# A gated mix of feature-map linear attention and a spatial gating unit: PE transposes for the first rows, v scaled in place of the key features, one PSUM pool, and a written TensorE order

## The chip, the cores and the metric

The kernel runs on one core of one Trainium2 chip. The metric is the time of one execution on the device in microseconds (us). PE is the engine of the matmuls, DVE, ACT and POOL are the vector, scalar and GpSimd engines, SP issues most of the transfers. Each engine runs its own instructions in order and waits for the others on semaphores.

## What is computed

x is 2048 x 512. Branch A is linear attention with 32 heads of 16 columns: softmax features of q and k (of +k w_phi and of -k w_phi), a sum of features times v over all rows, and a quotient. Branch B is a gated unit with 688 columns a half, whose second half is normalized and mixed over the rows. A gate per row mixes both.

```python
# A
phi_k = concat([softmax(pk), softmax(-pk)])      # pk = k @ w_phi, per head
kv = einsum('bhsf,bhsd->bhfd', phi_k, v); z = einsum('bhsf->bhf', phi_k)
o = einsum('bhqf,bhfd->bhqd', phi_q, kv) / (einsum('bhqf,bhf->bhq', phi_q, z) + 1e-6)
a = o @ wo
# B
z = gelu(x @ w_in); z1 = z[..., :688]; z2 = layernorm(z[..., 688:])
b = (z1 * (w_sp @ z2 + b_sp)) @ w_out
out = g * a + (1 - g) * b                        # g = sigmoid(sum(x * gate_w))
```

## The kernel before

Rows are worked on in 16 tiles of 128 (tt). The program has three stages. **z**: the x rows come transposed by DMA into xT (lines 92 to 106). In four chunks of four tiles, z2_tile multiplies the tile with the second half of w_in (and with gate_w as one more column, whose result DVE copies to glog), ACT takes the gelu, DVE the mean and variance; z1_tile does the first half; z2_norm normalizes the four tiles, with the power on POOL. zp, the PSUM result, has three buffers of two banks, and a buffer is free again when ACT's gelu and DVE's copy of the gate column have read it. DVE also casts bT (line 215), a bias that a DMA at the end of a long row of transposes on SP brings.

**Fold and kv**: w_phi is multiplied into wq and wk (lines 217 to 236), so that one product gives the exponents. For each tile kv_tile computes k and v, the exps of k and -k (ek), their sums a head (zk), the inverse (rk) and phik = ek rk; v is copied to vz with a column of ones behind it; kv_acc adds phik times vz into kvacc, which holds three banks through the stage. pq_tile does a fourth of the exps of q.

**Output**: gg_half multiplies the rows of w_sp with z2 in two halves of 344 columns (gp), and DVE forms ucat; attn_tile forms the quotient from eq and kvz (the masked kvacc); o and ucat are transposed by DMA (oT, uT); ba_tile adds both products (ba_ps), ACT scales and a DMA stores.

A scheduler of the framework sets the order of the instructions on every engine. PSUM has pools psA (z), psB (kv), psC (output) and psF throughout; psC begins where psB has ended.

## Time and profile before

| what | value |
|---|---|
| median of 3 runs | 237.82 us (237.62 to 238.41) |
| profiled execution | 236.93 us |
| its span, first to last instruction | 235.2 us |
| granted PE clock, mean | 0.993 |
| gp matmuls, 512 | 81.1 us busy, 313 ns each |
| z matmuls, 256 | 41.4 us busy, 324 ns each |
| wait of z for xT | 10.6 us of PE idle |

The span is what the trace covers; the rest of the execution's time lies around it. Busy times overlap on pipelined matmuls: a duration of 313 ns does not mean that one starts every 313 ns. What a matmul costs is read from the spacing of starts. In a row of the timeline the first number is the start and the second the duration in us; "x4" counts instructions merged into one row, and the bracket tells for how long the engine was idle ahead of it and what ended that. In rows of the groups the numbers are the total busy time, and the mean of one in ns.

### The profile page before, as it was taken

To read this page: it belongs to the slowest core of one execution; us is meant where nothing else is said; L and a number is where in the kernel's file an instruction comes from. 1 tells how busy PE (TensorE), PEld (TensorE's weight loads), DVE (VectorE), ACT (ScalarE), POOL (GpSimd) and SP (SyncE) were. 2 spreads that over 40 slices of the span, in tenths; PEclk is the share of its full clock that TensorE was granted. 3 is DMA by queue.
4 is the path that set the end of the run, shared out by engine and by line. 5 is a ranking of instruction groups with operands and counts; after the bars stand their busy time and mean duration, and the time that the engine had idled before them with its cause. 6 is when DMAs were issued, how large, how long until landed. Compare 5 with 4: busy or idle time off the path is not lost.

```text
span 235.2 us, 3568 instructions
## 1 busy us (share of the span) xinstructions
PE 212.9 (91%) x1412; PEld 127.9 (54%) x1412; DVE 149.0 (63%) x335; ACT 82.1 (35%) x133; POOL 9.9 (4%) x38
## 2 busy tenths in 40 slices
PE   0289999969999999995999999999999999999953
PEld 0046666645455555553675666666666566665611
DVE  0035747677999999997177745577455775556750
ACT  0126666694998888880001011110111101111011
POOL 7002021020000000000000000000000000000000
PEclk9999999999999999998899999999999999999999
DMA  7999999999900000000014234222333213322141
GB/s 139 203 220 256 253 189 283 241 200 267 261 3 0 0 3 0 0 0 3 1 34 84 52 78 81 56 52 51 78 78 59 55 47 79 81 57 54 48 100 45
DMA packets 72688, 22.29 MB, mean 95 GB/s; under 512 B 67888, under 2 KB 72672, under 8 KB 72672
## 3 DMA queue, kind: packets, MB, share of 16 engines
q1 hardware_dynamic: 71008, 20.64, 42.6%
q10 hardware_dynamic: 1632, 1.43, 3.2%
q8 instruction: 11, 0.18, 0.3%
q14 instruction: 5, 0.04, 0.1%
q0 software_dynamic: 32, 0.00, 0.0%
HBM read 3.18 MB, written 2.10 MB: 22 GB/s over the span
## 4 chain that ended last, share of the span: by engine, by line
PE 62%; DVE 28%; DMA 6%; issue 2%; ACT 1%; SPq 1%; POOLq 0%; DVEq 0%; POOL 0%; ACTq 0%
PE gp L371 32%; PE zp L172 14%; DVE phik L273 8%; PE ba_ps L391 8%; DVE zk L266 7%; PE ba_ps L389 5%; DMA xT<-in_A_x_dram 5%; DVE rk L271 4%; PE at L335 3%; DVE bn_83 L184 1%; DVE wk_p L236 1%; DVE wq_p L236 1%; DMA oT<-o 1%; DVE m L356 1%; DVE z2all L201 1%
## 5 line engine op out<-in xcount | busy, mean ns | idle before, releaser
L371 PE MATMUL gp<-z2all,wspT 128*128 128x344 bf16 x512 | 81.1, 313 | 0.8 <-DVE kvz L319 0.8
L371 PEld LDWEIGHTS <-wspT 128*128 128x128 bf16 x512 | 50.1, 99 | 26.8 <-issue 0.9
L393 ACT ACTIVATE ob<-ba_ps,g_inv 128x512 bf16<-128x512 f32 x16 | 11.0, 687 | 115.8 <-PE ba_ps L391 115.8
L172 PE MATMUL zp<-w_in,xT 128*128 128x344 bf16 (+1 forms) x256 | 41.4, 324 | 10.8 <-DMA xT<-in_A_x_dram 10.6
L172 PEld LDWEIGHTS <-xT 128*128 128x128 bf16 x256 | 25.6, 101 | 28.0 <-DMA xT<-in_A_x_dram 11.2
L391 PE MATMUL ba_ps<-w_out_t,uT 128*128 128x512 bf16 x96 | 23.3, 379 | 0.0
L273 DVE TENSOR_TENSOR phik<-ek,rk 128x1024 bf16<-128x1024 bf16 x16 | 19.6, 1223 | 1.3
L356 DVE TENSOR_TENSOR m<-at,r 128x1024 f32<-128x1024 f32 x16 | 19.6, 1224 | 0.5
L266 DVE TENSOR_REDUCE zk<-ek 128x64 f32<-128x1024 bf16 x16 | 19.3, 1209 | 0.0
L389 PE MATMUL ba_ps<-wo_t,oT 128*128 128x512 bf16 x64 | 16.6, 380 | 2.6 <-DMA oT<-o 2.6
L376 DVE SCALAR_TENSOR_TENSOR ucat_96<-gp,bT,z1all 128x344 bf16<-128x344 f32 x12 | 6.9, 571 | 18.8 <-PE gp L371 18.8
L181 ACT ACTIVATE z2all<-zp 128x688 bf16<-128x688 f32 x16 | 11.9, 744 | 15.2 <-PE zp L172 15.2
L253 PE MATMUL k_ps<-wk_p,xT 128*128 128x512 bf16 x64 | 16.9, 378 | 0.0
L256 PE MATMUL v_ps<-wv_sb,xT 128*128 128x512 bf16 x64 | 16.7, 379 | 0.0
L294 PE MATMUL pq<-xT,wq_p 128*128 128x512 bf16 x64 | 16.6, 379 | 0.0
L391 PEld LDWEIGHTS <-uT 128*128 128x128 bf16 x96 | 9.4, 98 | 11.2
L182 DVE COPY glog<-zp 128x1 f32<-128x1 f32 x16 | 2.5, 158 | 20.0 <-ACT z2all L181 19.8
L184 DVE BATCH_NORM_STATS2 bn_83<-z2all 128x6 f32<-128x344 bf16 x32 | 14.9, 501 | 0.0
L189 ACT ACTIVATE z1all<-zp 128x688 bf16<-128x688 f32 x16 | 11.7, 744 | 6.7 <-PE zp L172 6.7
L376 DVE SCALAR_TENSOR_TENSOR ucat_97<-gp,bT,z1all 128x344 bf16<-128x344 f32 x10 | 5.7, 570 | 13.0 <-PE gp L371 13.0
L376 DVE SCALAR_TENSOR_TENSOR ucat_98<-gp,bT,z1all 128x344 bf16<-128x344 f32 x10 | 5.7, 570 | 11.9 <-PE gp L371 11.9
L283 PEld LDWEIGHTS <-phik 128*128 128x128 bf16 x128 | 8.6, 98 | 6.1 <-DVE phik L273 2.8
(113 smaller groups left out, 197.4 us busy)
## 6 DMA issues: line engine op xcount, KB each, us to landing
out_dram<-ob SPq DMA_DIRECT2D x16, 128.0 KB, 1.9
w_in<-in_B_w_in_dram ACTq DMA_DIRECT2D x4, 172.0 KB, 4.3
w_in<-in_B_w_in_dram ACTq DMA_DIRECT2D x1, 688.0 KB, 10.2
w_out_t<-in_B_w_out_dram SPq DMA_DIRECT2D x1, 640.0 KB, 4.7
wv_sb<-in_A_wqkv_dram SPq DMA_DIRECT2D x1, 512.0 KB, 4.2
wo_t<-in_A_wo_dram SPq DMA_DIRECT2D x1, 512.0 KB, 5.2
oT<-o SPq DMA_TRANSPOSE x16, 2.5
uT<-ucat_96 SPq DMA_TRANSPOSE x6, 2.8
```

The source lines that it names most:

```text
L172: nc.tensor.matmul(zp[:, j, 0:n], lhsT=lhsT, rhs=w_in[:, dt, c0 + j * HF:c0 + j * HF + n], start=(dt == 0), stop=(dt == NDT - 1),)
L184: nc.vector.bn_stats(out=bn6[:, tt, j, :], in_=z2v[:, j, :])
L253: nc.tensor.matmul(k_ps[:, :], lhsT=xT[:, dt, t0:t0 + P], rhs=wk_p[:, dt, :], start=(dt == 0), stop=(dt == NDT - 1))
L256: nc.tensor.matmul(v_ps[:, :], lhsT=xT[:, dt, t0:t0 + P], rhs=wv_sb[:, dt, :], start=(dt == 0), stop=(dt == NDT - 1))
L266: nc.vector.tensor_reduce(out=zk[:, :], in_=ek[:].rearrange("p a (h e) -> p (a h) e", e=DH), axis=AX.X, op=ALU.add,)
L273: nc.vector.tensor_tensor(out=phik[:, :].rearrange("p (h e) -> p h e", e=DH), in0=ek[:].rearrange("p a (h e) -> p (a h) e", e=DH), in1=rk[ ...
L294: nc.tensor.matmul(pq[:, :], lhsT=wq_p[:, dt, g * P:(g + 1) * P], rhs=xT[:, dt, c0:c0 + CH], start=(dt == 0), stop=(dt == NDT - 1),)
L356: nc.vector.tensor_tensor(out=m[:].rearrange("p a (g h d) -> p (a g) h d", g=NG, d=DH), in0=at[:, :, :, 0:P].rearrange("p a g (h d) -> p ( ...
L371: nc.tensor.matmul(gp[:, :], lhsT=wspT[:, st, tt * P:(tt + 1) * P], rhs=z2all[:, st, j * HF:(j + 1) * HF], start=(st == 0), stop=(st == NT ...
L376: nc.vector.scalar_tensor_tensor(out=ucat[tt % NU][:, j * HF:(j + 1) * HF], in0=gp[:, :], scalar=bT[:, tt:tt + 1], in1=z1all[:, tt, j * HF ...
L389: nc.tensor.matmul(acc[:, :], lhsT=oT[:, g, :], rhs=wo_t[:, g, :], start=(g == 0), stop=False)
L391: nc.tensor.matmul(acc[:, :], lhsT=uT[:, ft, :], rhs=w_out_t[:, ft, :], start=False, stop=(ft == NFT - 1))
```

## The change

x rows 0 to 511 are loaded as they are (xs) and transposed on PE against an identity that DVE builds; gate_w is loaded as four rows and transposed on PE too. w_in becomes two tiles, loaded in pieces on SP and ACT. Eight matmuls on zeros stand first on PE. The folds stand between the z products of the last chunk, and every second result is copied by ACT. In the kv stage ek goes to kv_acc as it is; v is multiplied with rk once for each sign (vr, two DVE instructions from PSUM), and rk itself, copied by POOL, takes the place of the column of ones, so a kvacc block has 136 columns for 129. From kv to the end one pool psM serves all: four banks for k, v, pq, gp and the output products, four for kvacc and then at. The order on PE is the order of the code. The first gp half stands ahead of the last kv_acc; at of a tile follows its own gp halves, except for the last, where it stands between them. Stores go from ACT, and the last one is cut in two.

```diff
-    w_in = early.tile([P, NDT, F + 1], BF16, name="w_in")
+    w_z1 = early.tile([P, NDT, FH], BF16, name="w_z1")
+    w_z2 = early.tile([P, NDT, WP], BF16, name="w_z2")
...
-    NVZ = 4
-    vzs = [pers.tile([P, NG, P + 2], BF16, name=f"vz{i}") for i in range(NVZ)]
...
+    nc.vector.memset(warm[:], 0.0)
+    nc.vector.memset(ones32[:], 1.0)
...
+    for q in range(4):
+        qs = slice(32 * q, 32 * q + 32)
+        nc.vector.tensor_tensor(
+            out=ident[qs, qs], in0=ramp[qs, 0, :], in1=ramp[qs, 1, :], op=ALU.is_equal)
+    nc.gpsimd.dma_start(out=gaterow[:, :], in_=gate_w.rearrange("(dt p) -> dt p", p=P))
+    nc.sync.dma_start(out=xs[:, 0, :], in_=x2[0:P, :])
+    load_z2w(nc.scalar, 0)
+    load_z2w(nc.sync, 1)
+    load_z2w(nc.scalar, 2)
+    nc.sync.dma_start(out=xs[:, 1, :], in_=x2[P:2 * P, :])
+    load_z2w(nc.sync, 3)
+    nc.scalar.dma_start(
+        out=xs[:, 2:4, :], in_=x2[2 * P:4 * P, :].rearrange("(i p) d -> p i d", p=P))
+    for h in range(2):
+        nc.sync.dma_start(
+            out=w_z1[:, 2 * h:2 * h + 2, :], in_=w_in_v[:, 2 * h:2 * h + 2, 0:FH])
+    for i in range(4, 8):
+        nc.sync.dma_start_transpose(out=xT[:, :, i * P:(i + 1) * P], in_=x2[i * P:(i + 1) * P, :])
...
+    nc.scalar.dma_start(out=wphiE[:, :, :], in_=A_w_phi.rearrange("h e f -> e h f"))
...
-    def z_mm(tt, c0, w):
+    def z_mm(tt, wt, w, mid=None):
         zp = psA.tile([P, 2, CH], FP32, name="zp")
         for dt in range(NDT):
+            if dt == 2 and mid is not None:
+                mid()
...
+                    zp[:, j, 0:n], lhsT=lhsT, rhs=wt[:, dt, j * HF:j * HF + n],
...
-    def z2_tile(tt):
-        zp = z_mm(tt, FH, FH + 1)
+    def z2_tile(tt, mid=None):
+        zp = z_mm(tt, w_z2, FH + 1, mid)
...
-        zp = z_mm(tt, 0, FH)
+        zp = z_mm(tt, w_z1, FH)
...
-    for c in range(NCH):
-        ts = list(range(c * 4, c * 4 + 4))
-        for tt in ts:
-            z2_tile(tt)
-        for tt in ts:
-            z1_tile(tt)
-        z2_norm(ts)
-
-    nc.vector.tensor_copy(out=bT[:, :], in_=bT_bf[:, :])
...
+    def warm_up(n):
+        wp = psF.tile([P, CH], FP32, name="wp", tag="pq", bufs=2)
+        for _ in range(n):
+            nc.tensor.matmul(wp[:, :], lhsT=warm[:, 0:P], rhs=warm[:, :], start=True, stop=True)
+
+    def x_T(i):
+        tp = psF.tile([P, NDT, P], BF16, name="tp", tag="pq", bufs=2)
+        for dt in range(NDT):
+            nc.tensor.transpose(tp[:, dt, :], xs[:, i, dt * P:(dt + 1) * P], ident[:, :])
+        nc.vector.tensor_copy(out=xT[:, :, i * P:(i + 1) * P], in_=tp[:, :, :])
+
+    def gate_T():
+        gt = psF.tile([P, NDT], BF16, name="gt", tag="pq", bufs=2)
+        nc.tensor.transpose(gt[:, :], gaterow[:, :], ident[0:NDT, 0:NDT])
+        for dt in range(NDT):
+            nc.vector.tensor_copy(out=w_z2[:, dt, FH:FH + 1], in_=gt[:, dt:dt + 1])
+
+    def wphi_fold():
+        wps = psF.tile([P, NDT, P], FP32, name="wps", tag="pq", bufs=2)
+        for kc in range(NDT):
+            nc.tensor.matmul(
+                wps[:, kc, :], lhsT=eexp[:, :],
+                rhs=wphiE[:, kc * 8:(kc + 1) * 8, :].rearrange("e h f -> e (h f)"),
+                start=True, stop=True,
+            )
+        nc.vector.tensor_tensor(
+            out=wphi[:, :, :], in0=wps[:, :, :],
+            in1=mask_bd[:, None, :].to_broadcast([P, NDT, P]), op=ALU.mult,
+        )
+
...
+        if dt % 2 == 0:
+            nc.scalar.copy(out=dst[:, dt, :], in_=fps[:, :])
+        else:
             nc.vector.tensor_copy(out=dst[:, dt, :], in_=fps[:, :])
 
+    with tc.manual_schedule(engines={mybir.EngineType.PE}):
+        warm_up(8)
+        x_T(0)
+        gate_T()
+        for i in range(4):
+            z2_tile(i, (lambda k=i + 1: x_T(k)) if i < 3 else None)
+        for c in range(NCH):
+            ts = list(range(c * 4, c * 4 + 4))
+            last = c == NCH - 1
+            for tt in ts:
+                if c > 0:
+                    z2_tile(tt)
+                if last:
+                    fold(1, tt % 4)
+            for tt in ts:
+                z1_tile(tt)
+                if last:
+                    fold(0, tt % 4)
+            z2_norm(ts)
+            if c == NCH - 2:
+                wphi_fold()
...
+    psM = ctx.enter_context(
+        tc.tile_pool(name="psM", bufs=1, space=bass.MemoryType.PSUM, reuse_waits="tile"))
...
-    psB_cm = tc.tile_pool(name="psB", bufs=1, space=bass.MemoryType.PSUM, reuse_waits="tile")
-    psB = psB_cm.__enter__()
-    kvacc = [psB.tile([P, 3, P + 1], FP32, name=f"kvacc{i}") for i in range(3)]
-
-    def kv_tile(tt):
-        t0 = tt * P
-        k_ps = psB.tile([P, D], FP32, name="k_ps", bufs=2)
-        v_ps = psB.tile([P, D], FP32, name="v_ps", bufs=1)
+    kvacc = [psM.tile([P, NG, 256], FP32, name=f"kvacc{a}", tag="kvat", bufs=2) for a in range(2)]
...
+    def mm_tile():
+        return psM.tile([P, CH], FP32, name="mm", tag="mm", bufs=4)
+
+    def k_tile(tt):
+        k_ps = mm_tile()
...
-        vz = vzs[tt % NVZ]
-        nc.scalar.activation(
-            out=vz[:, :, 0:P], in_=v_ps[:, :].rearrange("p (g d) -> p g d", g=NG), func=AF.Copy,
-        )
+        ek = work.tile([P, 2, D], BF16, name="ek", bufs=4)
+        for a in range(2):
+            nc.scalar.activation(out=ek[:, a, :], in_=k_ps[:, :], func=AF.Exp, scale=1.0 - 2.0 * a)
...
-        phik = work.tile([P, 8 * P], BF16, name="phik", bufs=3)
...
+        return ek, rk
+
+    def v_tile(tt, rk):
+        v_ps = mm_tile()
+        for dt in range(NDT):
...
+        vr = work.tile([P, 2, NG, P + 8], BF16, name="vr", bufs=3)
+        nc.gpsimd.tensor_copy(
+            out=vr[:, :, :, P:P + 8], in_=rk[:].rearrange("p (a g h) -> p a g h", a=2, g=NG))
+        for a in range(2):
+            nc.vector.tensor_tensor(
+                out=vr[:, a, :, 0:P].rearrange("p g (h d) -> p g h d", d=DH),
+                in0=v_ps[:, :].rearrange("p (g h d) -> p g h d", g=NG, d=DH),
+                in1=rk[:, a * H:(a + 1) * H].rearrange("p (g h) -> p g h", g=NG)[:, :, :, None]
+                .to_broadcast([P, NG, 8, DH]),
+                op=ALU.mult,
+            )
+        return vr
+
+    def kv_acc(tt, ek, vr):
+        for a in range(2):
+            for g in range(NG):
+                nc.tensor.matmul(
+                    kvacc[a][:, g, 0:P + 8], lhsT=ek[:, a, g * P:(g + 1) * P], rhs=vr[:, a, g, :],
+                    start=(tt == 0 and g % 2 == 0), stop=(tt == NT - 1),
+                    skip_group_check=True,
+                )
...
-    pend = []
-    for tt in range(NT):
-        pend.append((tt,) + kv_tile(tt))
-        pq_tile(tt // 4, tt % 4)
-        if len(pend) > 2:
-            kv_acc(*pend.pop(0))
-    for p_ in pend:
-        kv_acc(*p_)
...
+    def kvz_evac():
+        for a in range(2):
+            nc.vector.tensor_tensor(
+                out=kvz[:, a * NG:(a + 1) * NG, 0:P], in0=kvacc[a][:, :, 0:P],
+                in1=mask_bd[:, None, :].to_broadcast([P, NG, P]), op=ALU.mult,
+            )
+            nc.vector.scalar_tensor_tensor(
+                out=kvz[:, a * NG:(a + 1) * NG, P:P + 8], in0=kvacc[a][:, :, P:P + 8],
+                scalar=0.5e-6, in1=mask8[:, None, :].to_broadcast([P, NG, 8]),
+                op0=ALU.add, op1=ALU.mult,
+            )
...
-        at = psC.tile([P, 2, NG, 256], FP32, name="at", bufs=1)
+        at = [psM.tile([P, NG, 256], FP32, name=f"at{a}", tag="kvat", bufs=2) for a in range(2)]
+        sd = work.tile([P, 2, NG, 16], FP32, name="sd")
...
-        sd = work.tile([P, 2, NG, 16], FP32, name="sd")
-        nc.vector.tensor_copy(out=sd[:], in_=at[:, :, :, P:P + 16])
+            nc.vector.tensor_copy(out=sd[:, a], in_=at[a][:, :, P:P + 16])
...
-        m = work.tile([P, 2, D], FP32, name="m", bufs=1)
-        nc.vector.tensor_tensor(
-            out=m[:].rearrange("p a (g h d) -> p (a g) h d", g=NG, d=DH),
-            in0=at[:, :, :, 0:P].rearrange("p a g (h d) -> p (a g) h d", d=DH),
-            in1=r[:].rearrange("p a g h -> p (a g) h")[:, :, :, None].to_broadcast([P, 8, 8, DH]),
-            op=ALU.mult,
-        )
+            nc.vector.tensor_tensor(
+                out=m[:, a].rearrange("p (g h d) -> p g h d", g=NG, d=DH),
+                in0=at[a][:, :, 0:P].rearrange("p g (h d) -> p g h d", d=DH),
+                in1=r[:, a][:, :, :, None].to_broadcast([P, NG, 8, DH]),
+                op=ALU.mult,
+            )
...
+        if tt < NT - 1:
+            nc.scalar.activation(out=ob[:, :], in_=acc[:, :], func=AF.Copy, scale=g_inv[:, tt:tt + 1])
+            nc.scalar.dma_start(out=out2[tt * P:(tt + 1) * P, :], in_=ob[:, :])
+        else:
+            hd = D // 2
+            nc.scalar.activation(out=ob[:, 0:hd], in_=acc[:, 0:hd], func=AF.Copy, scale=g_inv[:, tt:tt + 1])
+            nc.scalar.dma_start(out=out2[tt * P:(tt + 1) * P, 0:hd], in_=ob[:, 0:hd])
+            nc.vector.tensor_scalar(
+                out=ob[:, hd:D], in0=acc[:, hd:D], scalar1=g_inv[:, tt:tt + 1], scalar2=None, op0=ALU.mult)
+            nc.sync.dma_start(out=out2[tt * P:(tt + 1) * P, hd:D], in_=ob[:, hd:D])
+
+    nc.vector.tensor_copy(out=bT[:, :], in_=bT_bf[:, :])
...
-    for tt in range(NT):
-        gg_half(tt, 0)
-        if tt >= 1:
-            oTs[tt - 1] = attn_tile(tt - 1)
-        gg_half(tt, 1)
-        uTs[tt] = u_T(tt)
-        if tt == NT - 1:
-            oTs[tt] = attn_tile(tt)
-        if tt >= 2:
-            ba_tile(tt - 2, uTs.pop(tt - 2), oTs.pop(tt - 2))
-    for tt in (NT - 2, NT - 1):
-        ba_tile(tt, uTs.pop(tt), oTs.pop(tt))
-
-    psC_cm.__exit__(None, None, None)
+    with tc.manual_schedule(engines={mybir.EngineType.PE}):
+        ks = {0: k_tile(0)}
+        pend = []
+        for tt in range(NT):
+            if tt + 1 < NT:
+                ks[tt + 1] = k_tile(tt + 1)
+            ek, rk = ks.pop(tt)
+            pend.append((tt, ek, v_tile(tt, rk)))
+            pq_tile(tt // 4, tt % 4)
+            if len(pend) > 1:
+                kv_acc(*pend.pop(0))
+        nc.scalar.activation(out=g_el[:, :], in_=glog[:, :], func=AF.Exp)
+        nc.vector.tensor_scalar(out=g_1p[:, :], in0=g_el[:, :], scalar1=1.0, scalar2=None, op0=ALU.add)
+        nc.vector.reciprocal(out=g_inv[:, :], in_=g_1p[:, :])
+        gg_half(0, 0)
+        kv_acc(*pend.pop(0))
+        kvz_evac()
+        work_cm.__exit__(None, None, None)
+        work = ctx.enter_context(tc.tile_pool(name="workC", bufs=2, reuse_waits="tile"))
+        gg_half(0, 1)
+        uTs[0] = u_T(0)
+        oTs[0] = attn_tile(0)
+        for tt in range(1, NT):
+            gg_half(tt, 0)
+            if tt == NT - 1:
+                oTs[tt] = attn_tile(tt)
+            gg_half(tt, 1)
+            uTs[tt] = u_T(tt)
+            if tt < NT - 1:
+                oTs[tt] = attn_tile(tt)
+            if tt >= 2:
+                ba_tile(tt - 2, uTs.pop(tt - 2), oTs.pop(tt - 2))
+        for tt in (NT - 2, NT - 1):
+            ba_tile(tt, uTs.pop(tt), oTs.pop(tt))
 
```

Where the instructions stand now is shown at three places, first on DVE at the end of the first z chunk. Before (xT is written by DMA; z2all is the normalization of tiles 0 to 3, bT the cast, glog the gate copy of tile 4):

```order
L184 BN_STATS bn_83<-z2all 128x6
L185 BN_AGGR mv<-bn_83 128x2
L201 TENSOR_SCALAR z2all<-z2all,mv,rstd 128x688 x4
L215 CAST bT<-bT_bf 128x16
L182 COPY glog<-zp 128x1
L184 BN_STATS bn_83<-z2all 128x6 x2
```

After (the copy to xT empties the PE transpose of tile 3):

```order
L244 COPY xT<-tp 128x4x128
L213 BN_AGGR mv<-bn_84 128x2
L210 COPY glog<-zp 128x1
L212 BN_STATS bn_84<-z2all 128x6 x2
L229 TENSOR_SCALAR z2all<-z2all,mv,rstd 128x688 x4
L459 CAST bT<-bT_bf 128x16
```

The copies for xT came in ahead; the cast of bT stands where it stood, between the normalization and the gate copy of tile 4.

On ACT, the last z chunk. Before, the folds are not ACT's (g_el is the gate's exp, vz the copy of v):

```order
L312 ACT_TABLE_LOAD
L312 ACTIVATE g_el<-glog 128x16
L189 ACT_TABLE_LOAD
L189 ACTIVATE z1all<-zp 128x688 x4
L262 ACTIVATE vz_92<-v_ps 128x4x128
L259 ACT_TABLE_LOAD
L259 ACTIVATE ek<-k_ps 128x512
```

After:

```order
L276 CAST wk_p<-fps 128x512
L209 ACTIVATE z2all<-zp 128x688
L473 ACT_TABLE_LOAD
L473 ACTIVATE g_el<-glog 128x16
L217 ACT_TABLE_LOAD
L217 ACTIVATE z1all<-zp 128x688
L276 CAST wq_p<-fps 128x512
L217 ACTIVATE z1all<-zp 128x688 x2
L276 CAST wq_p<-fps 128x512
L217 ACTIVATE z1all<-zp 128x688
L323 ACT_TABLE_LOAD
L323 ACTIVATE ek<-mm 128x512 x4
```

Two fold copies came in between the gelus; the two loads around the gate's exp stayed; the exps of two k tiles follow at once.

On DVE, the start of the kv stage and its period. Before:

```order
L236 CAST wq_p<-fps 128x512 x4
L266 TENSOR_REDUCE zk<-ek 128x64
L271 RECIPROCAL rk<-zk 128x64
L273 TENSOR_TENSOR phik<-ek,rk 128x1024
L266 TENSOR_REDUCE zk<-ek 128x64
```

After:

```order
L325 TENSOR_REDUCE zk<-ek 128x64 x2
L330 RECIPROCAL rk<-zk 128x64 x2
L342 TENSOR_TENSOR vr<-mm,rk 128x4x128 x2
L325 TENSOR_REDUCE zk<-ek 128x64
L342 TENSOR_TENSOR vr<-mm,rk 128x4x128
L330 RECIPROCAL rk<-zk 128x64
L342 TENSOR_TENSOR vr<-mm,rk 128x4x128
```

Two tiles' zk and rk now precede the first vr, and later a vr of the tile before stands between zk and rk.

125 lines of the change are left out of this document (42 added, 83 removed).

## The prediction

> **What bounds the kernel now.** First the page's busy shares and slices, to see which engine is full in which stage.
>
> ```profile
> PE 212.9 (91%) x1412; PEld 127.9 (54%) x1412; DVE 149.0 (63%) x335; ACT 82.1 (35%) x133; POOL 9.9 (4%) x38
> PE   0289999969999999995999999999999999999953
> DVE  0035747677999999997177745577455775556750
> ```
>
> A slice is 5.88 us. PE is full except in the first three slices, near slice 9 (the fold), at slice 18 (the end of the kv stage) and in the last two. DVE is full beside PE in slices 9 to 17. So there is time to win only at the seams, and in the kv stage only if both engines get shorter. The timeline, engine by engine, gives the seams, each row as start, duration, instruction and the wait before it.
>
> ```profile
> 12.88 5.29 PE L172 MATMUL zp<-w_in,xT 128*128 128x344 bf16 x20 [5.28 <-DMA xT<-in_A_x_dram]
> 109.42 8.84 PE L371 MATMUL gp<-z2all,wspT 128*128 128x344 bf16 x48 [0.79 <-DVE kvz L319]
> 113.62 0.57 DVE L376 SCALAR_TENSOR_TENSOR ucat_96<-gp,bT,z1all 128x344 bf16<-128x344 f32 x1 [3.00 <-PE gp L371]
> 118.75 4.67 PE gp L371 x32
> 226.45 1.04 PE L389 MATMUL ba_ps<-wo_t,oT 128*128 128x512 bf16 x4 [2.08 <-DMA oT<-o]
> 229.28 1.04 PE L389 MATMUL ba_ps<-wo_t,oT 128*128 128x512 bf16 x4 [0.49 <-DMA oT<-o]
> ```
>
> PE starts z in earnest at 12.88. The first 16 gp matmuls run from 109.42 to about 113.55 (DVE takes their result at 113.62), 4.13 us, where the chain of waits has 32 in 4.67, so 2.33 for 16. At the end PE waits 2.08 and 0.49 for oT.
>
> **The start.** PE transposes replace the DMA transposes for rows 0 to 511, so z2 of tile 0 can begin as soon as plain loads land, far before 12.88. But all that is gained up to tile 7 hangs on one DVE row, and it did not move.
>
> ```profile
> 12.47 3.92 SPq L104 DMA_TRANSPOSE xT<-in_A_x_dram  x2
> 20.85 0.59 SPq L108 DMA_DIRECT2D wv_sb<-in_A_wqkv_dram  x1
> 21.49 1.13 SPq L112 DMA_TRANSPOSE bT_bf<-in_B_b_sp_dram  x1
> 25.49 0.17 DVE L215 CAST bT<-bT_bf 128x16 f32<-128x16 bf16 x1 [1.26 <-DMA bT_bf<-in_B_b_sp_dram]
> 25.75 0.16 DVE L182 COPY glog<-zp 128x1 f32<-128x1 f32 x1
> 28.50 0.74 ACT L181 ACTIVATE z2all<-zp 128x688 bf16<-128x688 f32 x1 [0.43 <-PE zp L172]
> 43.81 0.74 ACT L181 ACTIVATE z2all<-zp 128x688 bf16<-128x688 f32 x1 [0.44 <-PE zp L172]
> ```
>
> The cast of bT stands on DVE between the normalization of tiles 0 to 3 and the gate copy (glog) of tile 4, in both kernels. It waits for bT_bf, which lands at 25.45. Before, that cost DVE 1.26 us and PE nothing. After, PE comes there earlier: the gate copies of tiles 4, 5, 6 queue behind the cast, each holds one of the three zp buffers, and z2 of tile 7 cannot start until DVE has copied tile 4's gate. That is at 25.91, so landing plus 0.5.
>
> When bT lands now: SP issues the transposes of x rows 1024 to 2047 from 12.47, then wqkT, wv and bT, which lands 13.0 us after 12.47. That part is unchanged; what stands ahead of it is not. At best SP is limited by its own issue: six plain loads at 0.59 (wv's) and four 128-row transposes at 1.28 (the first x transpose, below) from 0.80 give 9.5, hence 22.4. At worst the bytes set it, which are the same ones (x, w_in, wqkv): 25.45. I take the middle, 24.0. Tile 7 then starts at 24.5 and ends at 25.7, where it ended just ahead of 28.50 less 0.07, at 28.43: **2.7 us gained** (1.3 to 4.2).
>
> Before that wait PE has little to do. By my count from 6 us (w_z2 landing; 4.3 us for each such load below), four z2 with transposes (6), four z1 (4.7) and z2 of tiles 4 to 6 (3.5) end near 20.5, at 1.18 a tile (28.50 to 43.81 is 13 tiles). PE then idles some 4 us.
>
> ```profile
> 0.80 1.28 SPq L92 DMA_TRANSPOSE xT<-in_A_x_dram  x1
> w_in<-in_B_w_in_dram ACTq DMA_DIRECT2D x4, 172.0 KB, 4.3
> 107.98 0.35 PE L283 MATMUL kvacc_633<-vz_95,phik 128*128 128x129 bf16 x3 [2.41 <-DVE phik L273]
> 112.00:113.00 1.00, 1.00 (x6) 0.53 0.00 0
> ```
>
> What such a gap does to the speed is seen twice. After the 5.28 us ahead of 12.88, 20 matmuls took 5.29, or 0.26 each where 0.146 is usual. After idling 2.41 and 0.79 us around eight short matmuls, PE was still granted 0.53 (the fourth column) between 112 and 113, and 16 matmuls took 4.13 in place of 2.33. The idle of 4 us lies between these, so I count **1.8 us lost** there (bounds 0 and 1.8). [...]
>
> **Fold, last z chunk and start of kv.** Take T as the moment when PE starts z2 of tile 12, its gelu at T + 1.24.
>
> ```profile
> 48.11 1.28 ACT L312 ACT_TABLE_LOAD   x1
> 49.63 1.28 ACT L189 ACT_TABLE_LOAD   x1
> 55.25 2.51 DVE L236 CAST wk_p<-fps 128x512 bf16<-128x512 f32 x4 [0.31 <-PE fps L230]
> 118.25 0.50 PE at L335 x8
> 57.46 1.28 ACT L259 ACT_TABLE_LOAD   x1
> 58.75 0.60 ACT L259 ACTIVATE ek<-k_ps 128x512 bf16<-128x512 f32 x1
> ```
>
> Each fold is four short matmuls, 0.24 (half of the eight at matmuls), and hides nothing, but moves into PE time beside z. The two table loads for the gate's exp stay in the last chunk. PE: four z2 and folds end at T + 5.65, two z1 and folds at 8.5, the third z1 at 9.6. The next fold needs the bank that ACT empties behind z1 of tile 12, and ACT comes to that only at 6.2 + 1.28 + 0.22 + 1.28 = 9.0, + 0.74 gelu + 0.67 copy = 10.4. Fold and last z1 end at 12.1. ACT then has two gelus, a copy and the last gelu: 13.2. k of tile 0 writes the bank of that last zp, so it starts at 13.2; Exp's load ends at 14.5, the exps of k0 and k1 at 15.7 and 16.9. DVE stands in the order zk0, zk1, rk0, rk1, vr0, so vr0 is ready at 20.4; PE has seven products (6.0) to do from 13.2 and waits for it from 19.2. kv_acc of tile 0 starts at T + 20.4.
>
> From there the stage is a period:
>
> ```profile
> 97.56 1.22 DVE L273 TENSOR_TENSOR phik<-ek,rk 128x1024 bf16<-128x1024 bf16 x1
> 98.70 1.21 DVE L266 TENSOR_REDUCE zk<-ek 128x64 f32<-128x1024 bf16 x1
> 99.95 0.55 DVE L271 RECIPROCAL rk<-zk 128x64 f32<-128x64 f32 x1
> 100.61 1.23 DVE L273 TENSOR_TENSOR phik<-ek,rk 128x1024 bf16<-128x1024 bf16 x1
> 98.14 0.34 PE L283 MATMUL kvacc_633<-vz_95,phik 128*128 128x129 bf16 x3
> 98.61 1.02 PE L253 MATMUL k_ps<-wk_p,xT 128*128 128x512 bf16 x4
> 99.47 1.03 PE L256 MATMUL v_ps<-wv_sb,xT 128*128 128x512 bf16 x4
> 100.34 1.03 PE L294 MATMUL pq<-xT,wq_p 128*128 128x512 bf16 x4
> L356 DVE TENSOR_TENSOR m<-at,r 128x1024 f32<-128x1024 f32 x16 | 19.6, 1224 | 0.5
> ```
>
> Before, DVE takes 3.05 a tile (97.56 to 100.61) and PE 0.47 + 3 x 0.86 = 3.05 too: both are full. After, PE has 136 columns for 129 in kv_acc: 0.48 + 2.58 = **3.06**. DVE exchanges phik (1.14 from start to start) for two vr of 512 from PSUM. No row has that form. Below stands m, from PSUM with a broadcast like it, half of 1224 or 0.61; above, the cast of 128x512 from PSUM, 2.51 / 4 = 0.63 a piece. With 0.62: 1.24 + 1.14 + 0.6 = 2.98, since zk's latency now lies behind a vr. PE sets the pace, barely. ACT loses the copy of v (0.6) and is not near. POOL's copy of rk is ready while DVE is at vr. From kv_acc 0 to the end of kv_acc 14: 15 x 0.48 + 41 x 0.86 = 42.5, so the first gp starts at T + 62.9, or 61.7 after the gelu of tile 12. Before it was 109.42 - 43.81 = 65.6. Less 0.24 for the wphi products ahead of T: **3.7 us gained** (PE-bound 4.0 at best; with vr at a full cast's 0.69, DVE at 3.12 a tile, 2.7).
>
> **The seam to the output.** gp needs no bank of kv any more and follows at once, so the slow clock at 109.42 is gone: **1.8 gained**. kv_acc of the last tile moves behind it: 0.48 lost. The four large kvz operations (two of 512, 0.63, two small) end 1.7 us after it, within the 2.33 of the second gp half, so at does not wait; without that cover 1.7 would show. The halves of at and m add two DVE instructions a tile to a stage where DVE is 60% busy; nothing waits.
>
> **The tail.** The row quotes 2.08 and 0.49 of waits; another 0.55 lies before the last at, which waited for m.
>
> ```profile
> 222.19 0.24 PEld L335 LDWEIGHTS <-eq_625 128*128 128x128 bf16 x4 [0.55 <-DVE m L356]
> 231.70 0.69 ACT L393 ACTIVATE ob<-ba_ps,g_inv 128x512 bf16<-128x512 f32 x1 [2.14 <-PE ba_ps L391]
> oT<-o SPq DMA_TRANSPOSE x16, 2.5
> ```
>
> Now the last at follows gp half 0 (end X). DVE finishes m at X + 3.7, then ucat 0.57, then o 0.68: X + 4.95. On SP oT stands behind uT (1.2 of issue), goes at X + 5.55 and lands 2.5 later, at X + 8.05. PE has gp half 1, two ba of 2.15 and at until X + 7.15. It waits 0.9 where it waited 3.1: **2.2 gained**. The last output, cut in two, saves half of 0.69: 0.3.
>
> **The sum.** 2.7 - 1.8 + 3.7 + 1.8 - 0.5 + 2.2 + 0.3 = 8.4 us off the profiled execution, 236.93 (span 235.2 and 1.73 around it): **228.5**. The median of the runs shown, 237.82, is 0.9 higher.
>
> **Rivals.** (1) The clock holds in the wait for bT, or bT comes before PE idles long: 1.8 less, 226.7; for it, after the idle of 1.92 us in these rows, eight z matmuls took 1.35 with the tail of the last, near their usual 1.17, so there is a length that does no harm. With bT at 22.4 as well, 225.1. [...]
>
> ```profile
> 52.96 0.21 PE L219 MATMUL wps<-wphiE,eexp 16*128 16x128 bf16 x1 [1.92 <-DVE wphi L224]
> 53.11 1.35 PE L172 MATMUL zp<-w_in,xT 128*128 128x344 bf16 x8
> ```
>
> (2) The start brings nothing: bT lands at 25.45 as before, since the bytes are the same: 229.9. If the wait of 1.2 before kv_acc 0, with 1.05 before k0, drops the clock also, 231.7. (3) DVE sets the kv pace at 3.12: 229.5. (4) Slower than before: PE now has a written order, so a late vr holds all that stands behind kv_acc (k, v and pq of the following tiles), where the old order was the scheduler's. It erases 8.4 us and 0.7 more if a tile takes 3.06 + 9.1 / 16 = 3.63, that is if a vr takes 0.95; at 1.0 the time is 239.4. The m row at 1224 for twice the columns speaks against it.
>
> **How the numbers follow.** Forecast (228.5, with 0.7 to either side for bT): 45%. Rival 1: 25%. Rival 2: 15%. Rival 3: 10%. Rival 4: 3%; 2% that gains and losses cancel. The range reaches from 224.5 (rival 1 with the early bT and a little of the tail) to 232 (rival 2 with the second slow clock). Faster by over 0.3%, which is about what a measurement here can tell: 95%; same 2%; slower 3%.
>
> **What would show it.** The cast of bT with several us of idle before it, z2 of tile 7 starting half a us behind, and a granted clock of 0.5 for some 3 us there: step one. A kv period near 3.06 with DVE at 2.98 and no idle on PE; vr at 0.62 from start to start. gp at full clock behind the last pq. A wait of 0.9 before the last ba. The forecast is wrong if PE passes tile 7 before 22, or if a kv tile takes over 3.2.

## The result, and the profile after

The changed kernel takes 231.5 us (median of 4 runs, 230.58 to 232.5), the kernel before 238.12 beside it: ratio 0.972, 95% interval 0.966 to 0.977. The profiled execution took 231.05. The forecast for it was 228.5, in a range of 224.5 to 232: it is faster, and by most of the steps named, but 2.5 us less than forecast. Its page:

```profile
span 229.2 us, 3683 instructions
PE 212.7 (93%) x1417; PEld 129.6 (57%) x1437; DVE 151.1 (66%) x382; ACT 76.3 (33%) x121; POOL 13.3 (6%) x50
PE   7895599996999999999999999999999999999972
DVE  3650548585799999997887655765557655666810
```

PE is now busy from the first slice, the dip of the nineteenth slice (the seam) is gone, and two new thin slices (the fourth and fifth) stand where z should run on. The timeline (start, duration, instruction, the wait before it and its releaser) has the places that the prediction named:

```profile
25.11 0.17 DVE L459 CAST bT<-bT_bf 128x16 f32<-128x16 bf16 x1 [7.60 <-DMA bT_bf<-in_B_b_sp_dram]
25.40 2.46 PE L200 MATMUL zp<-w_z_66,xT 128*128 128x344 bf16 x8 [4.82 <-DVE glog L210]
44.03 0.74 ACT L209 ACTIVATE z2all<-zp 128x688 bf16<-128x688 f32 x1 [0.86 <-PE zp L200]
44.81 0.16 DVE L210 COPY glog<-zp 128x1 f32<-128x1 f32 x1 [1.36 <-ACT z2all L209]
52.44 0.58 ACT L276 CAST wq_p<-fps 128x512 bf16<-128x512 f32 x1
53.16 0.68 DVE L278 CAST wq_p<-fps 128x512 bf16<-128x512 f32 x1
53.90 0.38 PE L269 MATMUL fps<-wphi,wqkT 128*128 128x128 bf16 x4 [1.55 <-DVE wq_p L278]
56.28 1.02 PE L319 MATMUL mm<-wk_p,xT 128*128 128x512 bf16 x3 [0.61 <-ACT z1all L217]
93.93 1.03 PE L319 MATMUL mm<-wk_p,xT 128*128 128x512 bf16 x4
95.86 0.69 DVE L342 TENSOR_TENSOR vr<-mm,rk 128x512 bf16<-128x512 f32 x1 [0.19 <-PE mm L336]
96.99 1.03 PE L319 MATMUL mm<-wk_p,xT 128*128 128x512 bf16 x3
105.32 2.50 PE L388 MATMUL mm<-z2all,wspT 128*128 128x344 bf16 x16
107.65 0.40 PE L354 MATMUL kvacc_682<-vr,ek 128*128 128x136 bf16 x4
213.69 0.41 PE L404 MATMUL at_2494<-kvz,eq_674 128*128 128x144 bf16 x4
219.13 1.22 SPq L433 DMA_TRANSPOSE oT<-o  x1
222.43 1.04 PE L444 MATMUL mm<-wo_t,oT 128*128 128x512 bf16 x4 [1.43 <-DMA oT<-o]
224.80 0.47 ACT L453 ACTIVATE ob<-mm,g_inv 128x256 bf16<-128x256 f32 x1 [3.08 <-PE mm L446]
225.31 0.48 DVE L455 TENSOR_SCALAR ob<-mm,g_inv 128x256 bf16<-128x256 f32 x1 [6.91 <-ACT ob L453]
```

The first two rows show PE standing 4.82 us behind DVE's gate copy, which stands behind the cast of bT. The k rows at 93.93 and 96.99 give the kv period, 3.06, and the vr row between them shows DVE waiting 0.19 for PE there, so PE sets that pace. The first gp (105.32) follows at full clock: 2.33 to the kv_acc at 107.65. The last rows show the end: oT lands 3.3 after its issue, and DVE's half of the last output runs behind ACT's. From starts like these, four stretches (the predicted gain is the sum of the prediction's terms in each):

| stretch | before | after | gained | predicted |
|---|---|---|---|---|
| start to gelu of tile 12 | 43.81 | 44.03 | -0.22 | 0.66 |
| to the first gp | 65.61 | 61.29 | 4.32 | 3.9 |
| to the last ba | 119.86 | 117.11 | 2.75 | 3.5 |
| to the end of the span | 5.92 | 6.77 | -0.85 | 0.3 |

The middle of the program did what was forecast; its two ends did not.

### The profile page after: what moved, and what is told of

Same layout as the page of the kernel before. It is cut to its first block, busy times and chain, and to the rows that moved or that the text cites. A ratio compares the mean times of both kernels' runs of the same rounds, so it can differ in the third digit from the quotient of the medians.

```text
span 229.2 us, 3683 instructions
## 1 busy us (share of the span) xinstructions
PE 212.7 (93%) x1417; PEld 129.6 (57%) x1437; DVE 151.1 (66%) x382; ACT 76.3 (33%) x121; POOL 13.3 (6%) x50
## 4 chain that ended last, share of the span: by engine, by line
PE 75%; SPq 8%; DVE 7%; DMA 5%; ACT 2%; issue 2%; POOL 1%
PE mm L388 32%; PE zp L200 8%; PE mm L446 8%; PE mm L336 5%; PE mm L364 5%; PE mm L444 5%; PE mm L319 5%; SPq L134 3%; SPq L129 2%; DMA bT_bf<-in_B_b_sp_dram 2%; PE kvacc_683 L354 2%; PE kvacc_682 L354 2%; SPq L131 2%; DVE bn_84 L212 1%; DMA oT<-o 1%
## 5 line engine op out<-in xcount | busy, mean ns | idle before, releaser
L388 PE MATMUL mm<-z2all,wspT 128*128 128x344 bf16 x512 | 77.6, 309 | 0.0
L200 PE MATMUL zp<-w_z_66,xT 128*128 128x344 bf16 (+1 forms) x128 | 22.1, 321 | 6.0 <-DVE glog L210 4.8
L446 PE MATMUL mm<-w_out_t,uT 128*128 128x512 bf16 x96 | 23.3, 379 | 0.0
L342 DVE TENSOR_TENSOR vr<-mm,rk 128x512 bf16<-128x512 f32 x32 | 21.5, 678 | 2.0 <-PE mm L336 1.9
L200 PE MATMUL zp<-w_z_65,xT 128*128 128x344 bf16 x128 | 20.4, 314 | 0.0
L323 ACT ACTIVATE ek<-mm 128x512 bf16<-128x512 f32 x32 | 17.3, 596 | 3.8 <-PE mm L319 3.8
L319 PE MATMUL mm<-wk_p,xT 128*128 128x512 bf16 x60 | 16.0, 379 | 0.8 <-ACT z1all L217 0.6
L336 PE MATMUL mm<-wv_sb,xT 128*128 128x512 bf16 x64 | 16.4, 379 | 0.0
L364 PE MATMUL mm<-xT,wq_p 128*128 128x512 bf16 x62 | 16.0, 379 | 0.0
L393 DVE SCALAR_TENSOR_TENSOR ucat_93<-mm,bT,z1all 128x344 bf16<-128x344 f32 x12 | 6.9, 575 | 13.7 <-PE mm L388 13.7
L393 DVE SCALAR_TENSOR_TENSOR ucat_95<-mm,bT,z1all 128x344 bf16<-128x344 f32 x10 | 5.8, 575 | 11.0 <-PE mm L388 11.0
L393 DVE SCALAR_TENSOR_TENSOR ucat_94<-mm,bT,z1all 128x344 bf16<-128x344 f32 x10 | 5.8, 575 | 11.0 <-PE mm L388 11.0
```

Source lines behind the costliest of these rows:

```text
L200: nc.tensor.matmul(zp[:, j, 0:n], lhsT=lhsT, rhs=wt[:, dt, j * HF:j * HF + n], start=(dt == 0), stop=(dt == NDT - 1),)
L319: nc.tensor.matmul(k_ps[:, :], lhsT=xT[:, dt, tt * P:(tt + 1) * P], rhs=wk_p[:, dt, :], start=(dt == 0), stop=(dt == NDT - 1))
L323: nc.scalar.activation(out=ek[:, a, :], in_=k_ps[:, :], func=AF.Exp, scale=1.0 - 2.0 * a)
L336: nc.tensor.matmul(v_ps[:, :], lhsT=xT[:, dt, tt * P:(tt + 1) * P], rhs=wv_sb[:, dt, :], start=(dt == 0), stop=(dt == NDT - 1))
L342: nc.vector.tensor_tensor(out=vr[:, a, :, 0:P].rearrange("p g (h d) -> p g h d", d=DH), in0=v_ps[:, :].rearrange("p (g h d) -> p g h d", g ...
L364: nc.tensor.matmul(pq[:, :], lhsT=wq_p[:, dt, g * P:(g + 1) * P], rhs=xT[:, dt, c0:c0 + CH], start=(dt == 0), stop=(dt == NDT - 1),)
```

## The experiments

Every kernel is the changed one with the edit shown; ratios are to the kernel before, timed on the same chip. What lies ahead of the gelu of tile 12 differs by 4 us from run to run (41.01 to 45.02 over the nine profiles with the PE transposes and the cast on DVE). Behind it, the stretches that an edit leaves alone repeat within 0.03 (to the first gp 61.28 or 61.29, from there to at of the last tile 108.36 or 108.37, in every run where they are unedited), so edits there are read from their stretch. The very end does not repeat like that, as the runs on the last output show.

**The cast of bT on POOL** (e1_bT_pool):

```diff
-    nc.vector.tensor_copy(out=bT[:, :], in_=bT_bf[:, :])
+    nc.gpsimd.tensor_copy(out=bT[:, :], in_=bT_bf[:, :])
```

> The cast of bT moves from VectorE to GpSimd; all else as after the change. Theory: the 4.82 us that TensorE waits ahead of z2 of tile 7 come from the gate copies queued behind that cast, and the slow clock behind it comes from this wait. Then z2 of tile 7 starts at about 20.6 in place of 25.40, its eight matmuls take 1.2 in place of 2.25, z2 of tile 8 starts at 26.4 in place of 32.89, and the span falls from 229.2 by 6.5 to 222.7. Rival A: the slow clock comes from the load at the start and not from the wait; then it shows at about 20 to 24 and the span is 224.4. Rival B: without the cast the next late thing is the x rows of tiles 8 to 15 (or wqkT); then z2 of tile 8 waits for DMA and the span is between 224 and 229. Rival C: GpSimd, now standing at the cast until 25.1, holds up the normalization of tiles 4 to 7, and TensorE waits there: z2 of tile 11 or 12 shows the wait.

Measured: 224.97 us, ratio 0.945 (0.940 to 0.949), profiled span 223.1, gelu of tile 12 at 37.86. In its timeline PE has no wait at tile 7 (its rows, from two windows that overlap, run on from 11.52 to 30), though bT lands no earlier, as POOL's row shows:

```profile
11.52 8.64 PE L200 MATMUL zp<-w_z,xT 128*128 128x344 bf16 x58 [0.77 <-DVE xT L244]
17.81 12.43 PE L200 MATMUL zp<-w_z,xT 128*128 128x345 bf16 x84
25.59 0.20 POOL L459 CAST bT<-bT_bf 128x16 f32<-128x16 bf16 x1 [9.21 <-DMA bT_bf<-in_B_b_sp_dram]
27.13 1.56 DVE L229 TENSOR_SCALAR z2all<-z2all,mv,rstd 128x688 bf16<-128x688 bf16 x4 [2.85 <-POOL rstd L227]
```

The theory holds: one copy of 0.17 us, put where it waited for a transfer, cost 6.2 us between these two profiles. The wait of 4.82 and the 1.65 of slow clock that the next run prices, less 0.46 by which z ran later here from its start on (the row at 11.52 stands at 11.06 in the changed kernel), make 6.0 of it. Rival C is seen in its mechanism (the normalization of tiles 4 to 7 waits for POOL, 2.85) but PE did not notice; rivals A and B fall.

**The gap filled with idle work** (e2_fill):

```diff
         for tt in ts:
+            if tt == 7:
+                warm_up(20)
             if c > 0:
                 z2_tile(tt)
```

> Twenty more warm-up matmuls of 128x512, whose result nobody reads, stand on TensorE ahead of z2 of tile 7; the wait for bT stays. It prices the clock alone. Theory: they fill 20.6 to 24.9, the gap before z2 of tile 7 is about 0.5, it starts at 25.4 as now, its eight matmuls take about 1.2 (2.25 now), z2 of tile 8 starts at 31.2 (32.89 now), span 227.6. Rival: the clock does not hang on the idle time; z2 of tile 7 is slow as before and the span stays at 229.2.

Measured: 229.63 us, ratio 0.965 (0.960 to 0.969), profiled span 227.7. The timeline, then the granted clock (the column after the engines) by windows of this run and of the changed kernel:

```profile
20.96 4.48 PE L238 MATMUL wp<-warm 128*128 128x512 bf16 x20
25.28 10.97 PE L200 MATMUL zp<-w_z,xT 128*128 128x344 bf16 x74
```

```profile
26.00:28.00 2.00, 2.00 (x16) 1.37 (x14) 1.93 (x9) 0.93 (x2) 0.00 (x0) 1.00 1.27 290
```

```profile
25.00:26.00 1.00, 0.60 (x3) 0.32 (x3) 0.89 (x4) 0.00 (x0) 0.00 (x0) 0.69 1.22 277
26.00:27.00 1.00, 1.00 (x5) 0.54 (x4) 0.96 (x5) 0.00 (x0) 0.00 (x0) 0.50 1.25 285
27.00:28.00 1.00, 1.00 (x5) 0.51 (x4) 0.97 (x5) 0.10 (x1) 0.00 (x0) 0.50 1.28 290
```

Tile 7 starts when it did (25.28 against 25.40) but from there to the gelu of tile 12 it is 16.98 in place of 18.63: the slow clock behind the gap costs 1.65. Matmuls whose result nobody reads bought that.

**The last output whole, or in two tiles** (e3_store_whole, e6_store_two):

```diff
-        if tt < NT - 1:
             nc.scalar.activation(out=ob[:, :], in_=acc[:, :], ...)
             nc.scalar.dma_start(out=out2[...], in_=ob[:, :])
-        else:
...
```

```diff
-                out=ob[:, hd:D], in0=acc[:, hd:D], scalar1=g_inv[...], ...)
+                out=ob2[:, :], in0=acc[:, hd:D], scalar1=g_inv[...], ...)
```

> The last output tile is scaled by ScalarE as a whole and stored by one transfer, as in the kernel before. Theory: the split cost time, since VectorE's half ran behind ScalarE's. From the start of ScalarE's operation to the end: 3.5 as in the kernel before, where the split shows 4.4; span 228.3. Rival: the end is set by how long a store takes to be complete and the split cost nothing: 229.2. Rival of the prediction: the split saves 0.3, and the span is 229.5.

> The last output tile stays split, but VectorE's half is written to a tile of its own. Theory: VectorE waited for ScalarE because both halves were written to one tile; with two, its half starts beside ScalarE's (224.8 in place of 225.31) and the span is 228.6 to 228.7. Rival: it waits because both read one accumulator in PSUM; then it starts behind ScalarE as now and the span stays at 229.2.

Measured: 230.77 us, ratio 0.970 (0.966 to 0.973), span 229.3; and 230.98, ratio 0.970 (0.966 to 0.974), span 229.5. The totals show no difference from the changed kernel; in these two profiles the gelu of tile 12 comes 1.0 and 0.2 later than in the changed kernel's, which hides what the end does. First the whole store's timeline, then the one with two tiles:

```profile
225.78 0.69 ACT L448 ACTIVATE ob<-mm,g_inv 128x512 bf16<-128x512 f32 x1 [3.08 <-PE mm L446]
226.50 0.34 ACTq L449 DMA_DIRECT2D out_dram<-ob  x1
```

```profile
225.01 0.47 ACT L453 ACTIVATE ob<-mm,g_inv 128x256 bf16<-128x256 f32 x1 [3.06 <-PE mm L446]
225.52 0.48 DVE L456 TENSOR_SCALAR ob<-mm,g_inv 128x256 bf16<-128x256 f32 x1 [6.90 <-ACT ob L453]
```

From ACT's start to the end of the span: whole 229.3 - 225.78 = 3.52, split 229.2 - 224.80 = 4.40, two tiles 4.49. So the split cost 0.9 in this pair of profiles, but that figure is one draw. Whole, the stretch is 3.5 in all three profiles that have it (before, e3_store_whole, e10_all). Split as in the changed kernel, it ranges from 3.73 (e5_phik) to 4.72 (e2_fill) over ten profiles, so the split cost 0.2 to 1.2. DVE's half is ready 0.3 later than a whole would be every time; the rest is its store on SP, whose time from issue to landing runs from 1.56 to 2.56, where a whole store, at the end of those three profiles, takes 1.70 or 1.71. Why that store varies is open. DVE waited for ACT with a tile of its own too, so the shared tile ob was not the reason. Both read the same accumulator in PSUM, and so do gelu and gate copy of a z2 tile, where DVE also starts when ACT ends. It starts 0.04 behind that end each time (225.31 against 224.80 + 0.47, 225.52 against 225.01 + 0.47, and 44.81 against 44.03 + 0.74 above). That the shared accumulator is the reason was not shown: a last tile with one accumulator for each half was not run.

**The gate's exp later** (e4_gate_late), **and one copy of the fold on ACT as well** (e9_gate_q1):

```diff
-        nc.scalar.activation(out=g_el[:, :], in_=glog[:, :], func=AF.Exp)
+            if tt == 2:
+                ...
+                nc.gpsimd.tensor_scalar(out=glog2[:, :], in0=rk[:, 0:NT], scalar1=0.0, ...)
+                nc.gpsimd.tensor_tensor(out=glog2[:, :], in0=glog2[:, :], in1=glog[:, :], op=ALU.add)
+                nc.scalar.activation(out=g_el[:, :], in_=glog2[:, :], func=AF.Exp)
+                ...
```

```diff
-        if dt % 2 == 0:
+        if dt % 2 == 0 or (qk == 0 and dt == 1):
             nc.scalar.copy(out=dst[:, dt, :], in_=fps[:, :])
```

> The exp of the gate moves from the last z chunk into the kv stage (two small GpSimd operations on its input tie it to rk of tile 2), so ScalarE has no table loads between z2 and z1 of the last chunk: 2 x 1.28 and 0.21 less on ScalarE there. Counted from the gelu of tile 12 to the first gp matmul, 61.29 now, since what lies ahead of it hangs on bT. Theory of the prediction: the fold of 1.55 wait stands behind ScalarE, so the wait goes, and the stretch falls by about 1.5 to 59.8. Rival: the fold waits for VectorE's cast of wq_p at 53.16, which stands behind three normalizations and these behind rstd at 52.05; ScalarE has nothing to do with it, the wait stays near 1.5 and the stretch at 61.0 to 61.3.

> As the kernel with the late gate exp, and the second fold of wq is copied out by ScalarE in place of VectorE. If the rival there is right (VectorE's order holds the fold), this removes the wait: z1 of tile 15 ends 1.4 to 1.5 earlier, and from the gelu of tile 12 to the first gp matmul it takes 59.7 to 60.0 (61.29 now). If the table loads held it, the late gate exp alone has already done this and here nothing more is gained. Third possibility: z1 of tile 15 comes earlier, but VectorE's normalizations, reductions and vr hold the first kv_acc, and the stretch falls by under 0.5.

Measured from the gelu of tile 12 to the first gp: 59.57 (41.01 to 100.58), and 59.58 with the further edit. So the late exp alone gains 1.72 and the further edit nothing: ACT's table loads were the cause, as the prediction had it, although the row of the wait (53.90, above) names DVE. The rival was read from that row and falls. In e4_gate_late DVE's cast of wq_p stands just where it stood, 9.1 after the gelu of tile 12 (50.13; 53.16 above), but the third fold runs at 49.16, ahead of that cast, so there it does not wait for DVE (why it does in the changed kernel is open); only the last fold waits, 0.16:

```profile
50.13 0.69 DVE L278 CAST wq_p<-fps 128x512 bf16<-128x512 f32 x1
...
49.16 0.39 PE L269 MATMUL fps<-wphi,wqkT 128*128 128x128 bf16 x4
50.87 0.38 PE L269 MATMUL fps<-wphi,wqkT 128*128 128x128 bf16 x4 [0.16 <-DVE wq_p L278]
```

The four runs of e4_gate_late spread from 225.53 to 230.0, so no ratio is given; its profiled run, the fastest, had the cast of bT at 23.74 and no slow clock behind it (last section). e9_gate_q1 took 229.65, ratio 0.958 (0.953 to 0.963).

**exp(k) scaled again** (e5_phik):

```diff
-        for a in range(2):
-            nc.vector.tensor_tensor(out=vr[:, a, :, 0:P]..., in0=v_ps[...], in1=rk[...], op=ALU.mult)
+        nc.scalar.activation(out=vz[:, :, 0:P], in_=v_ps[...], func=AF.Copy)
...
+        nc.vector.tensor_tensor(out=phik[...], in0=ek[...], in1=rk[...], op=ALU.mult)
```

> Undoes one part: exp(k) is scaled again (phik, VectorE, one operation of 1024 columns), and ScalarE copies v into tiles with columns of ones, as before the change; pool, order and widths stay. Theory: the scaling of v gained next to nothing, since VectorE had 3.05 a tile before and TensorE has 3.06 now: period 3.06 to 3.12, and from the first k matmul to the first gp matmul 49.0 to 50.0 (49.04 now). Rival: with phik three engines stand at 3.0 to 3.06 a tile (ScalarE takes 0.6 more for v) and do not fit into one another: period 3.2 to 3.3, that stretch 51.3 to 53.

Measured: 230.84 us, ratio 0.963 (0.958 to 0.968). From the first k (57.25) to the first gp (106.49) 49.24, against 49.04; the timeline shows the only wait and, from k to k, the period:

```profile
63.98 0.65 PE L356 MATMUL kvacc<-vz,phik 128*128 128x136 bf16 x8 [0.53 <-DVE phik L335]
95.10 1.03 PE L322 MATMUL mm<-wk_p,xT 128*128 128x512 bf16 x4
98.16 1.03 PE L322 MATMUL mm<-wk_p,xT 128*128 128x512 bf16 x4
```

The period is 3.06 either way: scaling v is worth 0.2 us here, since PE was the bound on both sides of that edit (DVE's wait of 0.19 a tile, above).

**The seam's order undone** (e7_seam):

```diff
-        gg_half(0, 0)
         kv_acc(*pend.pop(0))
         kvz_evac()
+        gg_half(0, 0)
```

> Undoes the order at the seam: kv_acc of the last tile and its four kvz operations stand ahead of the first gp half again. Counted from the gelu of tile 12 to at of the last tile (169.65 now, the same within 0.03 in every run so far that doesn't edit this stretch). Theory of the prediction: with kv_acc first, TensorE waits for the last vr (ready at 106.25 by the rows of the changed kernel, where it comes to it at 105.32): about 0.35 and 0.4, so the stretch is 170.3 to 170.5; the clock holds. Rival: such a pause with short matmuls in it slows the clock as at 109.42 before the change, and the stretch is 171.5 to 172.2. Rival: the order is worth nothing, 169.6.

Measured: 170.40 from the gelu of tile 12 (42.77) to at of the last tile (213.17), against 169.65, 0.75 more; 230.06 us, ratio 0.966 (0.961 to 0.971). The two waits are in the rows (idle time counted behind modelled ends, so their sum is less than the 0.75), and gp runs at full clock behind them:

```profile
104.45 0.41 PE L354 MATMUL kvacc<-vr,ek 128*128 128x136 bf16 x4 [0.23 <-DVE vr L342]
105.04 0.40 PE L354 MATMUL kvacc<-vr,ek 128*128 128x136 bf16 x4 [0.18 <-DVE vr L342]
105.27 4.83 PE L388 MATMUL mm<-z2all,wspT 128*128 128x344 bf16 x32
```

**The last o transposed by PE** (e8_oT_pe; four transposes and a DVE copy in place of the DMA transpose, ahead of the last two ba tiles):

```diff
+        tp = psM.tile([P, NG, P], BF16, name="tpo", tag="mm", bufs=4)
+        for g in range(NG):
+            nc.tensor.transpose(tp[:, g, :], o[:, g * P:(g + 1) * P], ident[:, :])
+        nc.vector.tensor_copy(out=oT[:, :, :], in_=tp[:, :, :])
```

> For the last tile alone, o is transposed by TensorE (four transposes between the last three ba products) and copied out by VectorE, in place of the DMA transpose. Theory: the wait of 1.43 before the last ba is the DMA's (from its issue 219.13 to 222.43, 3.3), queued 1.2 behind uT; it goes, the transposes cost 0.3 to 0.45. Counted from at of the last tile (213.69 now) to the last ba, 8.74 now, it falls to 7.5 to 7.7, and the end by 1.0 to 1.15. Rival: uT, issued at 217.83, lands hardly before 221.5, so the second part of the last ba waits in its place, and the end falls by under 0.5.

Measured: 229.51 us, ratio 0.959 (0.954 to 0.964). From at of the last tile (213.09) the last ba starts after 7.38, against 8.74, with no wait for uT either:

```profile
217.24 1.21 SPq L448 DMA_TRANSPOSE uT<-ucat  x1
218.51 0.42 DVE L443 COPY oT<-tpo 128x512 bf16<-128x512 bf16 x1 [0.71 <-PE tpo L441]
220.47 1.03 PE L454 MATMUL mm<-wo_t,oT 128*128 128x512 bf16 x4
```

1.36 gained, a little more than expected; the rival falls.

**The start undone** (e11_dma_xT; e12_dma_xT_pool has the cast on POOL as well; the matmuls on zeros and the transpose of gate_w stay):

```diff
-        x_T(0)
-            z2_tile(i, (lambda k=i + 1: x_T(k)) if i < 3 else None)
+            z2_tile(i)
...
+    nc.sync.dma_start_transpose(out=xT[:, :, 0:P], in_=x2[0:P, :])
+    nc.sync.dma_start_transpose(out=xT[:, :, P:CH], in_=x2[P:CH, :])
```

> Undoes the start alone: rows 0 to 511 of x come transposed by DMA, with the loads in the order of the kernel before; the cast of bT stays on VectorE. Theory: TensorE starts z near 12.9, has no wait ahead of tile 7 and no slow clock behind it, and the gelu of tile 12 starts at 43.9 to 44.3, where it started at 44.03 with the PE transposes; the PE transposes bought nothing because of the cast. Rival: they are worth the 0.9 of the prediction (2.7 less 1.8): 44.9 to 45.2. Rival: they are worth more, since the start now moves other transfers: over 45.5.

> The start undone as in the run beside it, and the cast of bT on GpSimd. Theory: with the late start nobody waits for the cast, so moving it alone changes nothing: gelu of tile 12 within 0.3 of the run beside it (about 44), where with the PE transposes moving it gained 6.2 (37.86). Rival: the cast costs by itself through VectorE's queue (its 1.26 of waiting before the change): then 1 to 1.3 earlier than the run beside it.

Measured: 232.96 us, ratio 0.979 (0.974 to 0.984), gelu of tile 12 at 44.86; and 231.67, 0.972 (0.967 to 0.978), at 45.54. That is 0.7 later than the run beside it, not within 0.3: PE's wait for w_in at the start took 4.90 there and 2.54 in the run beside it, and the slow clock lasted to 19.67, where full clock is on record from 17.09 in the other (the gelus of tiles 1 to 3 start at 16.70, 19.00 and 20.58 there, at 16.00, 17.79 and 18.95 in the other). My theory that the PE transposes bought nothing is not borne out: the profile gives 0.83 less without them, near the 0.9 of the prediction, and the medians 1.5 less. But the start with the transposes spreads over 41.01 to 45.02, so what they are worth stays open. With the late start, the cast on DVE held PE for 0.79 in the profile of e11_dma_xT (the last row), and that is the most that moving it could gain there; the medians, 232.96 and 231.67, come from runs that overlap, so a cost of the cast there is neither shown nor excluded. With the early start moving it brought 6.2. The rows of e11_dma_xT:

```profile
13.48 13.61 PE L192 MATMUL zp<-w_z,xT 128*128 128x344 bf16 x80 [2.35 <-DMA xT<-in_A_x_dram]
27.88 15.34 PE L192 MATMUL zp<-w_z,xT 128*128 128x344 bf16 x104 [0.79 <-DVE glog L202]
```

**Four findings together** (e10_all: cast on POOL, late gate exp, last o by PE, last output whole):

> The four findings together: cast of bT on GpSimd, late gate exp, o of the last tile transposed by TensorE, last output stored whole. Theory: they touch separate stretches and add up: gelu of tile 12 at 37.9, then 59.6 to the first gp, 108.36 to at of the last tile, 9.7 to the last operation of ScalarE, 3.5 to the end: span 219.1, time about 221, ratio to the kernel before about 0.928. Rival: an earlier part runs into something that the others hid (the weights of gp, landing in the kv stage, or uT of the last tile behind the stores): 220.5 or more.

Measured: 221.37 us, ratio 0.930 (0.926 to 0.934), the best of all kernels here, against a ratio of 0.972 for the changed one. The spans of five of its six runs are 218.7 to 219.8, as expected: the four gains add up. The profiled execution is the slowest of its six (223.55, span 221.6), and shows why its span is not 219.1: the stretches behind the gelu of tile 12 are 59.58, 108.36, 9.74 and 3.5, as expected, but that gelu comes at 40.42, not 37.9. The windows show a slow clock at the very start:

```profile
8.00:9.00 1.00, 0.59 (x3) 0.37 (x3) 0.09 (x1) 0.00 (x0) 0.00 (x0) 0.76 2.88 225
9.00:10.00 1.00, 1.00 (x5) 0.48 (x4) 0.00 (x0) 0.74 (x1) 0.00 (x0) 0.50 0.42 32
10.00:11.00 1.00, 1.00 (x7) 0.73 (x6) 0.30 (x1) 0.00 (x0) 0.00 (x0) 0.50 1.33 262
```

## The prediction, point by point

**The start** was right in its mechanism: the cast of bT, the gate copies behind it, tile 7 at once behind the landing, PE idle for some 4 us. The mis-sized term is the landing, "I take the middle, 24.0". It was 25.1 here, so the profiled run is close to rival 2's start. Over the nine profiles with the cast on DVE and the early start the cast runs between 23.74 and 25.74, with 24.82 in the middle: the forecast's 24.0 lies at the early side of what happens. The time of one profile is in part chance, since these nine reach the gelu of tile 12 up to 3.0 earlier and 1.0 later than the changed kernel's. SP was early as the lower bound assumed (the x rows up to 1023 were issued by 9.96); the lead went in the one issue of wqkT, which took 4.36 before the change, 4.56 in e4_gate_late and 6.55 in the changed kernel. Why it does is open.

**The slow clock**, 1.8 forecast, is 1.65 by e2_fill: right in size for this profile. The prediction chose between two values by the length of the pause; the last section shows that the length alone does not decide, and there the cost runs from 0 to 2.9.

**Fold, last chunk and kv.** Forecast 61.7 from gelu to gp, measured 61.29. PE's period of 3.06 and DVE within it were right, and so were ACT's table loads as the cause of the fold's wait (e4_gate_late). The bank was not: the forecast had the fold wait for the one that ACT empties, but ACT's copy had ended at 53.02 (52.44 + 0.58), and the fold started at 53.90, behind DVE's cast. The prediction let the kv gain seem tied to vr against phik; e5_phik prices that at 0.2. The rest of the 4.32 comes with the fold spread, the early k and the written order, which were not taken apart.

**The seam.** gp at full clock and one kv_acc behind it: right; e7_seam gives 0.75 for that order. The larger part, gp without the wait for banks, was not undone by itself. Before the change the clock fell there at 109.53, behind a window of 3.41 us in which PE was busy 0.76 (last section).

**The tail.** "Lands 2.5 later" was the page's median; the last oT took 3.3 after its issue behind uT's. With it the wait is 1.43 for 0.9, 0.5 short; e8_oT_pe shows that the wait is that transfer's. The other 0.25 that the stretch to the last ba lacks was not traced. **The last output**, "cut in two, saves half of 0.69", is wrong in kind: the two halves run one after the other, and the later one is ready 0.3 later than a whole would be (225.79 against 224.80 + 0.69). Its store then takes 3.4 from ready to the end in this profile, where the whole one's takes 2.8. It lost 0.9 where a gain of 0.3 was counted; in the ten profiles it lost 0.2 to 1.2, never gained.

So the 2.4 missing in the span are 0.9 at the start, 0.75 up to the last ba and 1.15 at the end, less 0.4 that kv gave more.

## What to carry to other kernels

When work is moved earlier, look for what stands in each queue between it and the rest: a small copy that waits for a late transfer was harmless while its engine was late, and became the largest loss found here when it was not. A wait's named releaser is the last event and not always the cause: the fold waited for DVE, and ACT's table loads were to be moved. Splitting an operation over two engines gained nothing here: the halves, which read one accumulator, ran one after the other (DVE 0.04 behind ACT's end), and the second store that it added took from 1.56 to 2.56 to land.
